# Zero matmuls in thin steps, loads in order of need, stages issued apart from their loads, and an early tail projection in a fused attention and long-convolution kernel

## Chip, cores, metric

One core of one Trainium2 chip runs the whole program. The metric is device time in microseconds (us), median of several executions. A span is the time from the first to the last instruction of the profiled execution; the measured time stands some 2 us above it.

Engines: PE does matmuls, ACT (ScalarE) exponentials, DVE (VectorE) copies out of the accumulators and small arithmetic, POOL (GpSimd) builds convolution operands, SP issues most DMAs. In these traces each starts its work in program order; that is why one wait can hold up what stands behind it (the prediction shows PE for 15.73 us at a convolution matmul, with the next scores behind it).

## The reference, cut

Two independent halves whose outputs are put side by side.

```python
# A: gated long convolution, S = 2048, D = 640
kv = shift(k, 4 taps) * v
y  = causal_convolution(kv, ssm_k) + kv * ssm_D      # by FFT in the reference
a  = q * y
# B: softmax attention, 32 heads of 20
qkv = x @ wqkv
p   = softmax(q @ k.T * 20**-0.5)
b   = (p @ v) @ wo
```

## The kernel before

One loop of 512 steps carries attention. A step `b` handles four heads (group `g`), one of 16 key blocks and one quarter of the queries: scores of four heads by four small matmuls, two exponentials of 128x1024, and PV, four matmuls that accumulate in one bank (`OBANK`) over 16 key blocks. Everything else is fitted into the holes of PE: transposes of x (`X`), the K, Q and V projections, normalisation (`N`), output projection (`T`, `O`), and the convolution as Toeplitz matmuls. All these share one bank, `MISC`, after the first steps.

```python
for b in range(NB):
    EXP_task(b)                                  # two exponentials on ACT
    if b + 1 < NB: S_task(b + 1)                 # scores; first runs the K and Q they need
    if b == 3: late[0] = 2                       # from here all filler uses bank MISC
    for m in (...[b - 1]): PV_task(m)            # first runs the V it needs
    bal = min(bal + (1.4 if b < 24 else 0.9), 1.2)
    if conv is None and kv_over and not any(e[3][0] in "XKV" for e in pend):
        conv_setup(); conv = conv_iter()         # issues loads, first use in the same step
    ... run pending tasks by deadline, else convolution matmuls, while bal lasts ...
    if b >= 6: micro(2)                          # kv product, later output stage A, on DVE
PV_task(NB - 1)
while pend: run_best()                           # tail: normalise, transpose, project, store
```

```python
def A_iter(B):                                   # output stage of the convolution
    A_load(B, 0); A_load(B, 1)
    for tp in range(8):
        ... DVE: Akv * D, + Y, * q ; store ; A_load(B, tp + 2)
```

Loads at the start: four tiles of x on SP, and beside them on ACT's queue the first 160 columns of each weight.

The softmax here doesn't subtract the row's maximum and nothing guards it: scores larger than these inputs give would overflow.

## Time and profile before

| | before |
|---|---|
| median of the first 3 runs | 1043.92 us (1041.96 to 1046.35) |
| span | 1040.8 us |
| mean granted clock of PE | 0.869 |
| first exponential starts | 17.75 us |
| last exponential ends, to the end of the span | 17.7 us |
| holes between exponentials, above 0.916 us from start to start | 67.2 us |

The last three rows and the undisturbed 938 us of exponentials make up the span. The mean clock counts time before the first clock record (24.5 us here) as full, though the transposes there run at the slow pace (20 in 2.31 us). The holes are worked out from the starts of the 1024 exponentials in the trace; the prediction shows the views.

### The profile page before, as it was taken

The page shows a single profiled execution, that of the slowest core. Times are in us where ns is not written, and L with a number is a line of the kernel's source. Part 1 is how long each engine was busy: PE and PEld are TensorE (multiplying, and loading weights), DVE is VectorE, ACT ScalarE, POOL GpSimd, SP SyncE. Part 2 cuts the span into 40 slices and gives each one's busy share as a digit, 9 for nine tenths or more (in the row PEclk, how much of TensorE's full clock was granted, in tenths as well). Part 3 has the DMA queues.
Part 4 walks back from the last instruction along what each step waited for, and adds up shares of the span by engine and source line. Part 5 has one row for each costly group of instructions (what it writes and reads, how often), then busy time and mean ns, then how long its engine had stood idle before and what let it go on. Part 6 is the DMA issues. An engine that isn't in the chain of part 4 may idle for free.

```text
span 1040.8 us, 25021 instructions
## 1 busy us (share of the span) xinstructions
PE 815.2 (78%) x11344; PEld 393.6 (38%) x11344; DVE 266.9 (26%) x568; ACT 949.9 (91%) x1033; POOL 119.1 (11%) x97
## 2 busy tenths in 40 slices
PE   5787888783887888988895888888888887666665
PEld 3332332221543555444452455544453553111112
DVE  3367776220112111121114311121112113200001
ACT  3579999993999999999997999999999999999994
POOL 3000000004220222220222022212220200000000
PEclk9679999996899999899998999999998997555556
DMA  9224443009880988563987578755573673100000
GB/s 353 75 90 144 159 142 112 4 1 145 178 189 31 204 188 182 126 137 94 199 199 181 144 180 191 170 132 134 128 171 91 137 174 98 46 1 1 1 1 26
DMA packets 74758, 129.05 MB, mean 124 GB/s; under 512 B 25729, under 2 KB 51451, under 8 KB 74651
## 3 DMA queue, kind: packets, MB, share of 16 engines
q1 hardware_dynamic: 71979, 124.09, 49.1%
q0 software_dynamic: 704, 2.74, 0.6%
q8 instruction: 89, 1.46, 0.6%
q10 hardware_dynamic: 1968, 0.61, 0.2%
q14 instruction: 18, 0.15, 0.1%
HBM read 116.81 MB, written 13.23 MB: 125 GB/s over the span
## 4 chain that ended last, share of the span: by engine, by line
ACT 76%; PE 15%; DVE 4%; DMA 2%; issue 1%; SPq 1%; POOL 1%; ACTq 0%
ACT P_sb L427 76%; PE PS L309 4%; PE PS L415 4%; PE PS L440 2%; PE PS L596 2%; PE PS L516 1%; PE PS L329 1%; DVE OT_sb L448 1%; DMA R<-in_B_wqkv_dram 1%; PE PS L461 1%; DMA R<-kvr_scratch 1%; DMA R<-kv_scratch 1%; SPq L144 1%; POOL R L573 1%; PE PS L289 0%
## 5 line engine op out<-in xcount | busy, mean ns | idle before, releaser
L427 ACT ACTIVATE P_sb<-PS 128x1024 bf16<-128x1024 f32 x1024 | 944.0, 1176 | 70.6 <-PE PS L415 67.4
L415 PE MATMUL PS<-QT,KT 20*128 20x512 bf16 x2048 | 227.3, 434 | 159.4 <-ACT P_sb L427 146.8
L596 PE MATMUL PS<-R 128*128 128x128 bf16 (+15 forms) x5120 | 219.8, 195 | 18.4 <-POOL R L573 15.7
L440 PE MATMUL PS<-P_sb,V_sb 128*21 128x512 bf16 x2048 | 226.4, 434 | 1.8 <-ACT P_sb L427 1.2
L596 PEld LDWEIGHTS PS<-R 128*128 128x128 bf16 x5120 | 194.0, 98 | 69.1 <-issue 53.1
L415 PEld LDWEIGHTS PS<-QT,KT 20*128 20x128 bf16 x2048 | 52.5, 92 | 295.3 <-ACT P_sb L427 277.8
L573 POOL COPY R<-R 32x512 bf16<-32x512 bf16 x80 | 106.9, 1337 | 473.0 <-PE PS L596 462.1
L440 PEld LDWEIGHTS PS<-P_sb,V_sb 128*21 128x21 bf16 x2048 | 50.5, 89 | 141.4 <-issue 137.2
L609 DVE CAST ZH<-PS 128x256 bf16<-128x256 f32 x40 | 17.0, 424 | 312.0 <-PE PS L596 311.9
L448 DVE CAST OT_sb<-PS 128x512 bf16<-128x512 f32 x32 | 22.1, 690 | 193.1 <-PE PS L440 193.0
L309 PE MATMUL PS<-xT,WQ 128*20 128x512 bf16 x640 | 49.1, 445 | 1.3 <-DVE O_norm L469 0.4
L309 PE MATMUL PS<-xT,R 128*20 128x512 bf16 x640 | 44.4, 411 | 6.1 <-DMA R<-in_B_wqkv_dram 4.1
L317 DVE CAST QT<-PS 128x512 bf16<-128x512 f32 x32 | 22.1, 692 | 57.5 <-PE PS L309 57.5
L329 PE MATMUL PS<-R,xT 128*128 128x160 bf16 (+1 forms) x240 | 34.4, 285 | 2.7 <-DVE V_sb L334 1.4
L317 DVE CAST KT<-PS 128x512 bf16<-128x512 f32 x32 | 22.1, 692 | 49.0 <-PE PS L309 49.0
L516 PE MATMUL PS<-Wo_sb,OnT 128*128 128x320 bf16 x160 | 30.0, 328 | 3.4 <-DVE OnT L507 1.8
L550 POOL MEMSET R<- 128x2048 bf16 x2 | 3.6, 1805 | 224.6 <-PE PS L309 224.5
L329 PEld LDWEIGHTS PS<-R,xT 128*128 128x128 bf16 x240 | 19.5, 108 | 18.7 <-DVE KT L317 4.4
L461 PE MATMUL PS<-ident,OT_sb 128*128 128x128 bf16 x128 | 14.6, 246 | 14.8 <-DVE OT_sb L448 14.8
L623 DVE CAST R<-PS 128x256 bf16<-128x256 f32 x40 | 17.0, 425 | 32.1 <-PE PS L617 32.1
L309 PEld LDWEIGHTS PS<-xT,WQ 128*20 128x20 bf16 x640 | 16.5, 100 | 22.8 <-issue 7.0
L309 PEld LDWEIGHTS PS<-xT,R 128*20 128x20 bf16 x640 | 15.6, 95 | 24.8 <-issue 8.0
(48 smaller groups left out, 285.6 us busy)
## 6 DMA issues: line engine op xcount, KB each, us to landing
R<-kext_scratch SPq DMA_DIRECT2D x320, 264.0 KB, 5.4
R<-in_A_k_dram SPq DMA_DIRECT2D x15, 640.0 KB, 3.8
R<-in_B_x_dram SPq DMA_DIRECT2D x4, 640.0 KB, 7.3
kext_scratch<-in_A_ssm_k_dram POOLq DMA_DIRECT2D x1, 2560.0 KB, 13.4
R<-in_A_v_dram SPq DMA_DIRECT2D x16, 160.0 KB, 5.4
kv_scratch<-R SPq DMA_DIRECT2D x16, 160.0 KB
kvr_scratch<-R SPq DMA_DIRECT2D x16, 160.0 KB
R<-kvr_scratch SPq DMA_DIRECT2D x8, 320.0 KB, 7.0
```

The costliest lines, as they stand in the source:

```text
L309: ins = e.matmul(bank[bk][32 * i:32 * i + DH, :], Wt[:, cc, off + i * DH:off + (i + 1) * DH], xT[:, cc, c * 512:(c + 1) * 512], start=(cc ...
L317: P.op("dve", lambda e: e.tensor_copy(dst, bank[bk]), reads=[bkb[bk]], writes=[bd])
L329: ins = e.matmul(bank[bk][:, 0:w], xT[:, cc, kb * 128:(kb + 1) * 128], WKV[:, cc, D + h0 * DH:D + h0 * DH + w], start=(cc == 0), stop=(cc ...
L415: ins = e.matmul(bank[bk], KT[32 * u:32 * u + DH, g, kb * 128:(kb + 1) * 128], QT[32 * u:32 * u + DH, qc % 2, g, :], start=True, stop=True ...
L427: P.op("act", lambda e, pr=pr, s0=s0: e.activation(P_sb[:, pr % NPS, :], PS[:, s0 * 512:s0 * 512 + 1024], ACT.Exp, scale=scale), reads=[bk ...
L440: ins = e.matmul(bank[OBANK][32 * u:32 * u + DH + 1, :], V_sb[:, kb, 4 * g + u, :], P_sb[:, (2 * b + u // 2) % NPS, (u % 2) * 512:(u % 2) ...
L448: P.op("dve", lambda e: e.tensor_copy(OT_sb[:, i, :], bank[OBANK]), reads=[bkb[OBANK]], writes=[b_OT[i]])
L461: ins = e.transpose(bankh[bk][:, qt * 128:(qt + 1) * 128], OT_sb[:, i, qt * 128:(qt + 1) * 128], ident)
L516: ins = e.matmul(bank[bk][:, 0:320], OnT[:, i, cc, :], Wo_sb[:, cc, hf * 320:(hf + 1) * 320], start=(cc == 0), stop=(cc == NCC - 1))
L573: P.op("pool", lambda e, dst=dst, src=src: e.tensor_copy(dst, src), reads=[cv["KVr"]], writes=[cv["KVX"][i]] if X == 3 else [], extra=(cv[ ...
L596: P.op("pe", lambda e, o=o, lhsT=lhsT, rhs=rhs, st=st, last=last: e.matmul(o, lhsT, rhs, start=st, stop=last, skip_group_check=True), read ...
L609: P.op("dve", lambda e: e.tensor_copy(zh, z1), reads=[bkb[MISC]], writes=[bz[0]])
```

## The change

It means to keep ACT at exponentials: by a warm clock (zeros), an earlier start (loads), loads issued well before the stage that uses them, and a short tail.

```diff
-        P.op("dve", lambda e: e.memset(bank[MISC], 0.0), writes=[bkb[MISC]])   # and three more banks
+        P.op("dve", lambda e: e.memset(Zt, 0.0), writes=[b_Zt])
+        def zeros(bk, n, start):
+            for _ in range(n):
+                P.op("pe", lambda e: e.matmul(bank[bk], Zt, zrhs, start=start, stop=start, ...), ...)
+        for bk in (7, 6, 0, 1, 2, 3, 4, 5, 7, 6):
+            zeros(bk, 1, True)
...
+        x_load(0)
+        w_load("act", 0, 160, b_Wa)
+        # x1 waits for the first weights; then x2, x3, the other weights
...
+        # tail: T tasks of the last quarter early with 4 of 5 chunks; tail_tasks() holds only
+        # the last PV, the last N, one chunk of transposes, and the projections
...
         def A_iter(B):
             A_load(B, 0)
             A_load(B, 1)
+            for _ in range(12):
+                yield
...
-            add(-10 if t < 4 else (t - 4) // 5, 0.45, ("X", t), ...)
+            add(-10 if t < 4 else (t - 4) // 2 if t < 8 else t - 6, 0.4, ("X", t), ...)
...
-            add(max(kb - 1, 2), 0.4, ("V", kb, 0), ...)
+            add(max(kb, 2), 0.41, ("V", kb, 0), ...)
...
+            if b < 40 and pend and min(pend)[2] < 0.45 and min(pend)[0] <= b + 6:
+                run_best()                       # one short task ahead of PV
...
-                conv = conv_iter()
+                conv, conv_b = conv_iter(), b + 10
...
-            if b >= 6:
+            if b >= 5 and stream < 0.35 and (b - 1) % NKB != NKB - 1:
+                zeros(OBANK, 2, False)
+            if b >= 18:
                 micro(2)
```

`stream` is the scheduler's own guess of how long PE streams filler in this step. There are 312 zero matmuls of 128x128 by 128x512: 10 at the start, 302 in the loop.

More of the change, by code (lines that the diff above doesn't have):

```diff
@@ L181, in build_kernel @@
         O_norm = sb("O_norm", [128, 4, D])
-        OnT = sb("OnT", [128, 2, NCC, 128])
+        OnT = sb("OnT", [128, 4, NCC, 128])
+        Zt = sb("Zt", [128, 128])
         Bout = sb("Bout", [128, 2, D])
@@ L239, in build_kernel @@
         b_On, b_rden = Buf(), [Buf(), Buf()]
-        b_OnT = [Buf(), Buf()]
+        b_OnT = [Buf() for _ in range(4)]
+        b_Zt = Buf()
         b_Bo = [Buf(), Buf()]
@@ L250, in build_kernel, with x_load, w_load @@
              reads=[b_ident], writes=[b_ident])
-        P.op("dve", lambda e: e.memset(bank[MISC], 0.0), writes=[bkb[MISC]])
-        P.op("dve", lambda e: e.memset(bank[0], 0.0), writes=[bkb[0]])
-        P.op("dve", lambda e: e.memset(bank[1], 0.0), writes=[bkb[1]])
-        P.op("dve", lambda e: e.memset(bank[OBANK], 0.0), writes=[bkb[OBANK]])
-        for n in range(4):
-            P.dma("sp", xst[n], ap(x2, [[D, 128], [128 * D, 4], [1, D]], n * 512 * D), DS("x%d" % n),
-                  writes=[b_xst[n]])
-        for eng, c0, w, bw in (("act", 0, 160, b_Wa), ("sp", 160, 480, b_Wb)):
+        P.op("dve", lambda e: e.memset(Zt, 0.0), writes=[b_Zt])
+        zrhs = ap(Zt, [list(Zt.ap[0]), [0, 4], [1, 128]])
+        def zeros(bk, n, start):
+            for _ in range(n):
+                P.op("pe", lambda e: e.matmul(bank[bk], Zt, zrhs, start=start, stop=start, skip_group_check=True),
+                     reads=[b_Zt], writes=[bkb[bk]], tok=start)
+        for bk in (7, 6, 0, 1, 2, 3, 4, 5, 7, 6):
+            zeros(bk, 1, True)
+        def x_load(n):
+            return P.dma("sp", xst[n], ap(x2, [[D, 128], [128 * D, 4], [1, D]], n * 512 * D), DS("x%d" % n),
+                         writes=[b_xst[n]])
+        def w_load(eng, c0, w, bw):
             P.dmas(eng, [(ap(t, [list(t.ap[0]), [t.ap[1][0], NCC], [1, w]], o + c0),
@@ L264, in build_kernel @@
                    DS("w" + eng), writes=[bw])
+        x_load(0)
+        w_load("act", 0, 160, b_Wa)
+        P.op("sp", lambda e: e.dma_start(xst[1], ap(x2, [[D, 128], [128 * D, 4], [1, D]], 512 * D)),
+             writes=[b_xst[1]], dsem=DS("x1"), extra=b_Wa.w)
+        x_load(2)
+        t_x3 = x_load(3)
+        w_load("sp", 160, 480, b_Wb)
         rot = [0]
@@ L395, in setup_pool @@
                 ap(kext, [[5 * KXL, 128], [KXL, 5], [1, KPAD]]),
-                ap(tB, [list(tB.ap[0]), [KPAD, 5], [1, KPAD]])), reads=[b_tB], writes=[b_kext], dsem=d_kext)
+                ap(tB, [list(tB.ap[0]), [KPAD, 5], [1, KPAD]])), reads=[b_tB], writes=[b_kext], dsem=d_kext,
+                extra=[t_x3])
             P.op("pool", lambda e: e.dma_start(
@@ L456, in N_task @@
             i = g % 2
-            bk = mbank2()
+            bk = MISC
             def pe(e):
@@ L472, in N_task @@
                 reads=[bkb[bk], b_rden[i]], writes=[b_On])
-            if g == NG - 1:
+            if g == NG - 2 and qc == NQC - 1:
+                for qt in range(4):
+                    add(NB - 12 + 2 * qt, 0.4, ("T", qc, qt), lambda qt=qt: OnT_task(qc, qt, 0, 4))
+            if g == NG - 1 and qc < NQC - 1:
                 b0 = (qc + 1) * 128
@@ L479, in N_task, with OnT_task @@
                             lambda qt=qt, hf=hf: O_task(qc, qt, hf))
-        b_OnT4 = [b_OnT[0], b_OnT[1]]
-        d_B = [DS("b0"), DS("b1")]
-        def OnT_task(qc, qt):
-            if qt >= 2:
+        d_B = [DS("b%d" % i) for i in range(4)]
+        def OnT_task(qc, qt, c0=0, c1=NCC):
+            if qc > 0:
                 for hf in range(2):
-                    ensure(("O", qc, qt - 2, hf))
-            elif qc > 0:
-                for hf in range(2):
-                    ensure(("O", qc - 1, qt + 2, hf))
-            i = qt % 2
-            bk = mbank2()
+                    ensure(("O", qc - 1, qt, hf))
+            bk = MISC
             def pe(e):
-                for cc in range(NCC):
+                for cc in range(c0, c1):
                     ins = e.transpose(bankh[bk][:, cc * 128:(cc + 1) * 128], O_norm[:, qt, cc * 128:(cc + 1) * 128],
@@ L499, in OnT_task @@
             P.op("pe", pe, reads=[b_On, b_ident], writes=[bkb[bk]])
-            evac(OnT[:, i, :, :], bankh[bk][:, 0:640].rearrange("p (c n) -> p c n", c=NCC), bk, b_OnT[i])
+            evac(OnT[:, qt, c0:c1, :], bankh[bk][:, c0 * 128:c1 * 128].rearrange("p (c n) -> p c n", c=c1 - c0), bk,
+                 b_OnT[qt])
         def evac(dst, src, bk, bd):
@@ L507, in evac, with O_mm, pe, O_store @@
                 P.op("dve", lambda e: e.tensor_copy(dst, src), reads=[bkb[bk]], writes=[bd])
+        def O_mm(qt, hf, bk, c0=0, c1=NCC):
+            def pe(e):
+                for cc in range(c0, c1):
+                    ins = e.matmul(bank[bk][:, 0:320], OnT[:, qt, cc, :], Wo_sb[:, cc, hf * 320:(hf + 1) * 320],
+                                   start=(cc == 0), stop=(cc == NCC - 1), skip_group_check=True)
+                return ins
+            P.op("pe", pe, reads=[b_OnT[qt], b_Wo], writes=[bkb[bk]])
+        def O_store(qc, qt, src, bd):
+            P.dma("sp", ap(out2, [[2 * D, 128], [1, D]], (qc * 512 + qt * 128) * 2 * D + D), src, d_B[qt], reads=[bd])
         def O_task(qc, qt, hf):
@@ L511, in O_task, with tail_tasks @@
             i = qt % 2
-            bk = mbank2()
+            O_mm(qt, hf, MISC)
+            evac(Bout[:, i, hf * 320:(hf + 1) * 320], bank[MISC][:, 0:320], MISC, b_Bo[i])
+            if hf == 1:
+                O_store(qc, qt, Bout[:, i, :], b_Bo[i])
+        def tail_tasks():
+            qc, g = NQC - 1, NG - 1
+            tail[0] = True
+            for hf in range(2):
+                O_mm(0, hf, 2 + hf, 0, 4)
+            PV_task(NB - 1)
+            for hf in range(2):
+                O_mm(1, hf, 4 + hf, 0, 4)
+            ensure(("N", qc, g))
+            for hf in range(2):
+                O_mm(2, hf, hf, 0, 4)
             def pe(e):
-                for cc in range(NCC):
-                    ins = e.matmul(bank[bk][:, 0:320], OnT[:, i, cc, :], Wo_sb[:, cc, hf * 320:(hf + 1) * 320],
-                                   start=(cc == 0), stop=(cc == NCC - 1))
-                return ins
-            P.op("pe", pe, reads=[b_OnT[i], b_Wo], writes=[bkb[bk]])
-            evac(Bout[:, i, hf * 320:(hf + 1) * 320], bank[bk][:, 0:320], bk, b_Bo[i])
-            if hf == 1:
-                P.dma("sp", ap(out2, [[2 * D, 128], [1, D]], (qc * 512 + qt * 128) * 2 * D + D), Bout[:, i, :], d_B[i],
-                      reads=[b_Bo[i]])
-        tail = [False]
-        def mbank2():
-            if tail[0]:
-                rot[0] += 1
-                return (MISC, 0, 1, 2, 3, 4, 5)[rot[0] % 7]
-            return MISC
+                for qt in range(4):
+                    ins = e.transpose(bankh[OBANK][:, qt * 128:(qt + 1) * 128], O_norm[:, qt, 512:640], ident)
+                return ins
+            P.op("pe", pe, reads=[b_On, b_ident], writes=[bkb[OBANK]])
+            P.op("dve", lambda e: e.tensor_copy(OnT[:, :, 4, :],
+                                                bankh[OBANK][:, 0:512].rearrange("p (t n) -> p t n", t=4)),
+                 reads=[bkb[OBANK]], writes=b_OnT)
+            for qt, bks, c0 in ((0, (2, 3), 4), (1, (4, 5), 4), (2, (0, 1), 4), (3, (MISC, OBANK), 0)):
+                Bt, bd = P_sb[:, qt, 0:D], b_P[qt]
+                for hf in range(2):
+                    O_mm(qt, hf, bks[hf], c0, NCC)
+                    evac(Bt[:, hf * 320:(hf + 1) * 320], bank[bks[hf]][:, 0:320], bks[hf], bd)
+                O_store(qc, qt, Bt, bd)
+        tail = [False]
         cv = {}
@@ L679, in build_kernel @@
         for t in range(NKB):
-            add(-10 if t < 4 else (t - 4) // 5, 0.45, ("X", t), lambda t=t: XT_task(t))
+            add(-10 if t < 4 else (t - 4) // 2 if t < 8 else t - 6, 0.4, ("X", t), lambda t=t: XT_task(t))
         for g in range(NG):
@@ L687, in build_kernel @@
         for kb in range(NKB):
-            add(max(kb - 1, 2), 0.4, ("V", kb, 0), lambda kb=kb: V_task(kb, 0))
+            add(max(kb, 2), 0.41, ("V", kb, 0), lambda kb=kb: V_task(kb, 0))
             add(18 + kb, 0.4, ("V", kb, 1), lambda kb=kb: V_task(kb, 1))
@@ L718, in build_kernel @@
         S_task(0)
-        conv, conv_over = None, False
+        conv, conv_over, conv_b = None, False, NB
         locked = False
@@ L724, in build_kernel @@
         bal = 0.0
+        stream = 0.0
         def micro(n):
@@ L740, in build_kernel @@
                 late[0] = 2
+            bal = min(bal + (1.3 if b < 24 else 0.9), 1.2)
+            nm, stream = 0, 0.0
+            if b < 40 and pend and min(pend)[2] < 0.45 and min(pend)[0] <= b + 6:
+                run_best()
+                bal -= 0.4
             for m in ([] if b < 3 else [2 * b - 6, 2 * b - 5] if b < 5 else [b - 1]):
                 PV_task(m)
-            bal = min(bal + (1.4 if b < 24 else 0.9), 1.2)
             if conv is None and kv_over and not any(e[3][0] in "XKV" for e in pend):
                 conv_setup()
-                conv = conv_iter()
-            nm = 0
+                conv, conv_b = conv_iter(), b + 10
             if not locked:
-                while pend and nm < (6 if b < 3 else 2 if b < 16 else 1) and (bal > 0.5 or b < 3):
+                while pend and nm < (2 if b < 16 else 1) and bal > 0.4:
                     if min(pend)[0] > b + (40 if b < 128 else 10):
                         break
-                    bal -= run_best()
+                    c = run_best()
+                    bal -= c
+                    stream += 0.8 * c
                     nm += 1
-            if nm == 0 and conv is not None and not conv_over:
+            if nm == 0 and b >= conv_b and not conv_over:
                 while bal > 0:
@@ L762, in build_kernel @@
                         bal -= r
+                        stream += 0.7 * r
                     elif r == "wait":
@@ L767, in build_kernel @@
                         bal -= 0.5
+                        stream += 0.4
                         if r[1] in (19, 39):
@@ L770, in build_kernel @@
                         break
-            if b >= 6:
+            if b >= 5 and stream < 0.35 and (b - 1) % NKB != NKB - 1:
+                zeros(OBANK, 2, False)
+            if b >= 18:
                 micro(2)
-        PV_task(NB - 1)
-        tail[0] = True
-        while pend:
-            run_best()
-        if conv is None:
-            conv_setup()
-            conv = conv_iter()
-        for r in conv:
-            if isinstance(r, tuple) and r[1] in (19, 39):
-                acts.append(A_iter(r[1] // 20))
-        while acts:
-            micro(1)
-        fin = [d[2] for d in d_B + d_ao if len(d) > 2]
+        assert not [e for e in pend if e[3] != ("N", 3, 7)] and conv_over and not acts
+        tail_tasks()
+        fin = [d[2] for d in d_B + d_ao]
         waits = [(t[2], t[1]) for t in fin]
```

## The prediction

> **What bounds the kernel now.** I first read the page. ScalarE (ACT) is busy in 91% of the span, the chain that ended last lies on its exponentials for 76%, and all 1024 of them are one line.
>
> ```profile
> PE 815.2 (78%) x11344; PEld 393.6 (38%) x11344; DVE 266.9 (26%) x568; ACT 949.9 (91%) x1033; POOL 119.1 (11%) x97
> ...
> ACT  3579999993999999999997999999999999999994
> ...
> PEclk9679999996899999899998999999998997555556
> ...
> L427 ACT ACTIVATE P_sb<-PS 128x1024 bf16<-128x1024 f32 x1024 | 944.0, 1176 | 70.6 <-PE PS L415 67.4
> ```
>
> The tenths of ACT show where it is not full: the first three slices, the tenth, the 22nd and the last. The last column of the exponentials says what it waited for: scores (L415). Undisturbed runs give the real price of one: 168 in 154.45 us, less one instruction's 1.176 at the end, over 167 distances, is 0.918 us start to start (the 1176 ns overlap); shorter runs give 0.912. I use 0.916. So a step of the loop (two exponentials) is 1.83 us, and 1024 exponentials need 1023 x 0.916 + 1.18 = 938 us whatever else happens. The span is 1040.8, so 103 us can be had at most. The timeline of ACT says where they are:
>
> ```profile
> 17.75 3.77 ACT L427 ACTIVATE P_sb<-PS 128x1024 bf16<-128x1024 f32 x4 [9.28 <-PE PS L415]
> 23.88 1.94 ACT L427 ACTIVATE P_sb<-PS 128x1024 bf16<-128x1024 f32 x2 [2.36 <-PE PS L415]
> ...
> 258.58 1.94 ACT L427 ACTIVATE P_sb<-PS 128x1024 bf16<-128x1024 f32 x2 [16.09 <-PE PS L415]
> ...
> 277.63 154.45 ACT L427 ACTIVATE P_sb<-PS 128x1024 bf16<-128x1024 f32 x168 [0.58 <-PE PS L415]
> ...
> 559.99 1.94 ACT L427 ACTIVATE P_sb<-PS 128x1024 bf16<-128x1024 f32 x2 [6.00 <-PE PS L415]
> ```
>
> The first exponential starts at 17.75 and the last ends at 1023.1, so head 17.75, tail 17.7, and between them 1005.3 - 938.2 = 67 us of holes. Summing the excess of each start-to-start distance over 0.916 us by stage: 21.9 us up to 72.6; 6.6 to 240; 16.7 at 258; 2.2 to 278; 4.8 to 549; 7.3 at 560; 4.7 to 875; 3.0 after it (total 67.2).
>
> The two big holes have one shape: PE's queue is in order, and it stands at an instruction whose data has just been asked for, while the next scores stand behind it.
>
> ```profile
> 239.89 5.72 SPq L144 DMA_DIRECT2D R<-kvr_scratch  x4
> 250.71 11.07 POOL L573 COPY R<-R 32x512 bf16<-32x512 bf16 x8 [7.19 <-DMA R<-kvr_scratch]
> 256.26 1.73 PE L596 MATMUL PS<-R 128*128 128x128 bf16 x21 [15.73 <-POOL R L573]
> ...
> 556.91 0.49 DVE L641 TENSOR_TENSOR R<-R,Dbc 128x640 bf16<-128x640 bf16 x1 [7.56 <-DMA R<-kv_scratch]
> ```
>
> Loads of the convolution are issued at 239.9, its copies on GpSimd start at 250.7, its first matmul at 256.3. At 556.9 VectorE, also in order, stood 7.56 us at a load of the output stage; a normalisation and transpose that PE needed were behind it.
>
> The small holes are mostly cold clock. Windows:
>
> ```profile
> 25.00:50.00 25.00, 19.60 (x183) 8.53 (x183) 9.32 (x24) 15.00 (x17) 0.00 (x0) 0.69 0.30 94
> 175.00:200.00 25.00, 19.90 (x292) 6.56 (x288) 9.81 (x18) 25.00 (x29) 0.00 (x0) 1.00 0.05 18
> 900.00:1000.00 100.00, 63.34 (x444) 12.62 (x440) 5.76 (x12) 98.14 (x107) 0.00 (x0) 0.50 0.00 1
> ```
>
> (us; PE, PEld, DVE, ACT, POOL busy; granted clock; DMA share; GB/s.) With a K or Q projection in most steps and the clock at 1.00, ACT has no hole at all (175 to 200). A projection's 20 matmuls span 2.31 us cold and 1.25 warm; cold it alone exceeds a step. At 900 to 1000 the clock is half throughout and ACT is still 98% busy: thin steps (scores and PV, 0.61 us each when cold) do not need the clock.
>
> **The Trainium skill.** "TensorE: Matmul & The Clock Gate", Part 1: the clock has a half and a full rate, judged in free-running windows of 3.4 us of activity, and gaps make it cold. The trace agrees on the rates and windows (cold stretches last 3.41 us or multiples) but not that only idleness counts: taking each matmul as its columns at the granted clock, I find that all 18 drops to half rate follow a window with PE streaming 16 to 45% of the time, and all 18 rises one with 77 to 90%. "PSUM — Partial Sum Buffer", The four PSUM rules: a matmul without the first-flag adds where the bank was written, so zeros leave PV as it is, and one with the flag can take over from the four VectorE memsets; a time trace cannot show values. "ScalarE: Activation LUTs", What ACT_TABLE_LOAD costs: 186 ns + 0.833 per element, 93 ns overlapped, gives 946 ns; the trace's 0.912 to 0.918 is less, and is used. "DMA: Bandwidth & Descriptors", Why small descriptors are slow: small packets move less per unit of time. The DMA view of the first 30 us agrees:
>
> ```profile
> q1 hardware_dynamic: 5306, 6.41, 62.6%
> q10 hardware_dynamic: 1968, 0.61, 8.1%
> ```
>
> Of 16 x 30 us, a packet of q10 (the first weights, 320 B each by their shape) takes 20 ns, one of q1 57 ns.
>
> **The change part by part.** From the instruction order of both builds; steps are counted by scores.
>
> *Loads.* Before, x0 to x3 (2.6 MB) share the engines with the first weights (0.6 MB), which end at 11.7 us. Now only x0 does: packet time (512 x 57 + 1920 x 20) / 16 = 4.2 us, begun at about 2, so they land near 7 (estimate). x0's 20 transposes take 5.4 to 7.7 and their copies to 8.5 as before, and now gate. Then K and Q: 4.45 us cold, 2.3 warm, plus 1.46 from Q's end to the first exponential. The ten zero matmuls (about 1.2 to 5.5, cold 0.427 each) may warm the clock: 12.2 warm, 14.4 cold; I take 13.0. **Gain 4.8.**
>
> *Early steps (to about step 30).* The kv product on VectorE starts 12 steps later, x transposes are spread, and zeros lift a thin warm step from 0.43 to 0.85 us of streaming per 1.83, 46%: just over the 45% at which the last drop happened; cold they make 1.71, 93%, enough to rise. I go through steps 3 to 29 with warm durations: scores and PV 0.33 each to the next issue, projection 1.1, V about 0.33, zeros 0.43, and 0.45 or 0.76 where PE waits for a V or K copy. Step 7 has V, wait, PV, transposes, zeros, then K for the very next scores and its copy: about 4.0 us against 1.83, a hole of 2. Steps 4, 5 and 11 lose about 1 each, other steps to 10 about 0.5, and 13, 14, 16, 19, 24, 29 (V and a projection) about 0.6. With the slack of about 0.3 us in a step that is 13. **Gain 9.**
>
> *Clock elsewhere.* Half of the zeros lie after step 432, where only the boundary steps lose (0.46 us each): gain 1.5. Holes of 1.2 us at cold projections from 72 us on should shrink: 6.6 to 2, 2.2 to 0.5, 4.8 to 1.5, 4.7 to 1.5. **Gain 14.3 with the end.**
>
> *Convolution.* Loads, clearing and copies are issued 10 steps, 18.3 us, before the first matmul; the chain needed 16.4 (239.84 to 256.26). **Gain 15.7**, leaving 1.
>
> *Output stage.* 12 rests at two per step are 11 us, the load took 7.1. **Gain 6.3.**
>
> *Tail.* Now four of five transposes and projections per row tile stand ready. From the last exponential: PV 0.5, copy 0.7, one more projection holding PE (to 1.5), transposes 0.4, reciprocal and multiply 0.85, transposes and copy 1.1, then 16 matmuls and eight copies of 0.44 to 0.49 on two engines to about 7.2, and the 2.2 us that the store and the end took before: 9.5. **Gain 8.2.**
>
> Sum: 4.8 + 9 + 14.3 + 15.7 + 6.3 + 8.2 = 58.3. The other way: 13.0 + 938.2 + 22 of holes (13 + 2 + 1 + 0.5 + 1.5 + 1 + 1.5 + 1.5) + 9.5 = 982.7 of span; the median stands 3.1 above the span, so 985.8.
>
> **Rivals.** *Zeros make PE the bound.* 302 zeros in the loop at 0.43 us cold are at most 130 us of PE. A cold thin step becomes 0.54 + 0.54 + 0.86 = 1.94 us against 1.83. If the clock flickers there, 151 steps lose up to 0.1: 15 us back, about 1000. Against: the step itself rises to 93%. *Early stage stays bound by waits.* The steps before 12 still put V right before the PV that needs it; if the clock stays cold there the 9 us shrink to about 0: 995. *The wait moves.* Ten steps leave only 2 us of margin for the loads; a slower load shows a few us of hole: 990. Conversely, if early steps hide the copies better than I think: 975. *Nothing gained because ACT sets the pace anyway:* against it speaks that the 67 us are holes in ACT itself.
>
> **Range and chances.** The convolution, output stage and tail (30 us) follow from single visible waits and are nearly sure; head and clock (28 us) may come at a third or at full with something over. So 974 to 1003. Faster by 2% needs 1023: all but certain.
>
> **What would show it.** Right: first exponential at 12 to 14.5; no hole over 3 us at the convolution or output stage; granted clock near 1.0 after 880 us; zero matmuls outside every chain; last exponential to end 9 to 10.5. Wrong: a clock of 0.5 to 0.8 with zeros present, ACT's distance in steady runs above 0.92, or early holes above 18 us.

## The result

The changed kernel took 1000.98 us (993.27 to 1006.58, 4 runs), the kernel before 1043.59 us in the same rounds: ratio 0.9584, 95% interval 0.9504 to 0.9664. (A ratio is the mean time of one kernel's runs over that of the other's of the same rounds, so not quite the ratio of the medians.) The span of the profiled run is 994.7 us. The time lies inside the predicted range, 15 us above the predicted figure, and its spread of 13 us is new: the kernel before spreads by 4 us here and by 5 to 7 in the sets below.

The page of the changed kernel, the same lines as before (PE as a whole, ACT and granted clock in 40 slices, the exponentials):

```profile
PE 834.1 (84%) x11656; PEld 398.7 (40%) x11656; DVE 266.8 (27%) x568; ACT 947.5 (95%) x1031; POOL 118.9 (12%) x97
...
ACT  4578999999999999999999999999999999999996
...
PEclk7799999999999999999999999999999999999989
...
L446 ACT ACTIVATE P_sb<-PS 128x1024 bf16<-128x1024 f32 x1024 | 943.4, 1239 | 34.6 <-PE PS L434 29.7
```

ACT is full from the fifth slice to the last but one, and the clock is high everywhere but at the start. What is left is the start: its tenths, 4 5 7 8, are no better than before (3 5 7 9). The timeline of ACT shows it (start, duration, what; idle time before, and who ended it):

```profile
11.01 7.44 ACT L446 ACTIVATE P_sb<-PS 128x1024 bf16<-128x1024 f32 x8 [3.68 <-PE PS L434]
22.53 1.94 ACT L446 ACTIVATE P_sb<-PS 128x1024 bf16<-128x1024 f32 x2 [4.09 <-PE PS L459]
...
40.37 1.94 ACT L446 ACTIVATE P_sb<-PS 128x1024 bf16<-128x1024 f32 x2 [4.49 <-PE PS L434]
42.78 1.94 ACT L446 ACTIVATE P_sb<-PS 128x1024 bf16<-128x1024 f32 x2 [0.47 <-PE PS L434]
...
195.32 343.42 ACT L446 ACTIVATE P_sb<-PS 128x1024 bf16<-128x1024 f32 x374 [0.20 <-PE PS L434]
...
544.90 415.24 ACT L446 ACTIVATE P_sb<-PS 128x1024 bf16<-128x1024 f32 x452 [0.33 <-PE PS L434]
```

The first exponential starts 6.7 us sooner. Then come holes of up to 4.5 us until 40 us, and of 0.2 to 1.6 us, mostly about 0.5, in most steps until 95. From 195 us on, the 374 and 452 exponentials of the two stretches shown run almost without a hole; the holes of 16 and 6 us are gone.

Holes by steps (sum of the excess over 0.916 us, from the trace):

| steps | before | changed | what lies there |
|---|---|---|---|
| 0 to 30 | 22.7 | 28.1 | x, first K, Q, V |
| 30 to 96 | 4.4 | 4.6 | more K, Q, V |
| 96 to 110 | 18.0 | -0.2 | start of the convolution |
| 110 to 256 | 7.1 | 0.2 | convolution |
| 256 to 290 | 7.1 | 0.8 | first output stage |
| 290 to 432 | 4.9 | 0.2 | convolution |
| 432 to 512 | 3.0 | 2.2 | scores and PV alone |
| all | 67.2 | 35.9 | |

With the first exponential (17.75 to 11.01) and the tail (17.7 to 9.4) this is 6.7 + 31.3 + 8.3 = 46.3, and the span fell by 46.1.

**The convolution.** Timeline lines from SP, POOL and PE, the same events as before:

```profile
217.37 5.66 SPq L144 DMA_DIRECT2D R<-kvr_scratch  x4
...
229.96 11.09 POOL L615 COPY R<-R 32x512 bf16<-32x512 bf16 x8 [8.98 <-DMA R<-kvr_scratch]
...
236.04 1.35 PE L638 MATMUL PS<-R 128*128 128x128 bf16 x33
```

The chain is no shorter, 12.6 us from issue to first copy (10.8 before) and 18.7 to the first matmul (16.4 before), but PE no longer stands in it: its matmul line names no wait. It was close: the first tile's four copies end at 235.46 in the trace, 0.6 us before PE arrives.

**The output stage.** The waits of DVE for this load (total, times, longest):

```profile
DVE R L685 <- DMA R<-kv_scratch: 13.5, 11, 2.5
```

Before, the longest was 7.56 us; 2.5 does not reach ACT.

**The start.** Timeline of the first weights' user and what it waited for:

```profile
5.26 1.29 PE L307 MATMUL PS<-ident,R 128*128 128x128 bf16 x20 [0.22 <-DMA R<-in_B_x_dram]
...
7.06 0.39 SPq L278 DMA_DIRECT2D R<-in_B_x_dram  x1
...
7.43 1.26 PE L327 MATMUL PS<-xT,R 128*20 128x512 bf16 x20 [0.88 <-ACT xT L315]
```

The second x tile is issued at 7.06, when the first weights have landed (before, they were waited for until 11.84), and the first projection then waits for copies of x, not for weights. It takes 1.26 us, so the clock is warm.

**The tail.**

```profile
985.72 0.40 PE L459 MATMUL PS<-P_sb,V_sb 128*21 128x512 bf16 x4
...
987.14 0.39 PE L480 MATMUL PS<-ident,OT_sb 128*128 128x128 bf16 x4
...
988.88 0.42 DVE L563 COPY OnT<-PS 128x512 bf16<-128x512 bf16 x1 [0.53 <-PE PS L560]
...
991.74 0.49 DVE L525 CAST P_sb<-PS 128x320 bf16<-128x320 f32 x1 [0.21 <-PE PS L530]
```

The last exponential ends at 985.3, the last copy at 992.2, the span at 994.7: 9.4 us.

**The clock.** Windows (us; PE, PEld, DVE, ACT, POOL busy; granted clock; DMA share; GB/s) of the changed kernel:

```profile
16.00:39.00 23.00, 20.01 (x143) 8.07 (x139) 5.11 (x12) 10.20 (x11) 0.68 (x1) 0.51 0.82 274
39.00:64.00 25.00, 19.73 (x235) 8.19 (x231) 8.10 (x18) 17.72 (x19) 0.00 (x0) 1.00 0.00 1
850.00:950.00 100.00, 71.16 (x550) 17.49 (x550) 10.22 (x21) 99.74 (x110) 0.00 (x0) 0.95 0.07 19
```

Late, the clock is 0.95, where the kernel before has 0.60 in the same stretch and the changed kernel without the loop's zeros (second run below) 0.50. Early, from 15 to 39 us, it is half, and ACT is busy for 10.2 of 23 us. Even from 39 to 64 us, with the clock full, ACT is busy in only 17.7 of 25 us. So two theories for the early holes: the cold clock, or waits that any clock has. Around 28 us PE, DVE and PE again do this:

```profile
26.86 0.85 PE L347 MATMUL PS<-R,xT 128*128 128x160 bf16 x5
27.75 0.33 DVE L352 CAST V_sb<-PS 128x160 bf16<-128x160 f32 x1 [0.94 <-PE PS L347]
28.13 0.61 PE L459 MATMUL PS<-P_sb,V_sb 128*21 128x512 bf16 x4 [0.42 <-DVE V_sb L352]
```

V is projected right before the PV that reads it, and PE stands still until DVE has copied it. The page adds this up:

```profile
L459 PE MATMUL PS<-P_sb,V_sb 128*21 128x512 bf16 x2048 | 206.2, 393 | 4.2 <-DVE V_sb L352 4.2
```

In the kernel before PV waited for V's copy once, for 0.4 us; here ten times, for 4.2 us in all. The change itself is the likely maker: it put V's deadline one step later (`kb - 1` became `kb`). No run alters this alone.

### The profile page after: what moved, and what is told of

The parts are those of the page before. It is cut to its first block, busy times and chain, and to the rows that moved or that the text cites. A ratio compares the mean times of both kernels' runs of the same rounds, so it can differ in the third digit from the quotient of the medians.

```text
span 994.7 us, 25641 instructions
## 1 busy us (share of the span) xinstructions
PE 834.1 (84%) x11656; PEld 398.7 (40%) x11656; DVE 266.8 (27%) x568; ACT 947.5 (95%) x1031; POOL 118.9 (12%) x97
## 4 chain that ended last, share of the span: by engine, by line
ACT 83%; PE 10%; DVE 4%; DMA 1%; issue 1%; SPq 0%
ACT P_sb L446 83%; PE PS L327 3%; PE PS L434 2%; PE PS L347 2%; PE PS L459 1%; PE PS L259 1%; DVE V_sb L352 1%; DVE KT L335 1%; PE PS L530 1%; PE PS L307 1%; DMA R<-kv_scratch 1%; DVE OT_sb L467 0%; DMA R<-in_B_x_dram 0%; PE PS L480 0%; DVE R L387 0%
## 5 line engine op out<-in xcount | busy, mean ns | idle before, releaser
L434 PE MATMUL PS<-QT,KT 20*128 20x512 bf16 x2048 | 205.4, 391 | 126.6 <-ACT P_sb L446 113.4
L638 PE MATMUL PS<-R 128*128 128x128 bf16 (+15 forms) x5120 | 214.5, 193 | 2.6 <-DVE QT L335 1.2
L459 PE MATMUL PS<-P_sb,V_sb 128*21 128x512 bf16 x2048 | 206.2, 393 | 4.2 <-DVE V_sb L352 4.2
L638 PEld LDWEIGHTS PS<-R 128*128 128x128 bf16 x5120 | 189.1, 97 | 51.1 <-issue 51.1
L259 PE MATMUL PS<-Zt 128*128 128x512 bf16 x312 | 99.5, 405 | 1.0 <-DVE Zt L253 1.0
L327 PE MATMUL PS<-xT,R 128*20 128x512 bf16 x640 | 42.0, 393 | 2.6 <-ACT xT L315 0.9
L327 PE MATMUL PS<-xT,WQ 128*20 128x512 bf16 x640 | 41.2, 387 | 1.0 <-DVE O_norm L488 0.4
L259 PEld LDWEIGHTS PS<-Zt 128*128 128x128 bf16 x312 | 21.0, 100 | 26.9 <-issue 25.9
L530 PE MATMUL PS<-Wo_sb,OnT 128*128 128x320 bf16 x160 | 26.6, 301 | 0.7 <-DVE OnT L563 0.5
L352 DVE CAST V_sb<-PS 128x160 bf16<-128x160 f32 (+1 forms) x48 | 18.3, 382 | 24.8 <-PE PS L347 24.0
```

What stands on the lines that cost most here:

```text
L259: P.op("pe", lambda e: e.matmul(bank[bk], Zt, zrhs, start=start, stop=start, skip_group_check=True), reads=[b_Zt], writes=[bkb[bk]], tok=s ...
L327: ins = e.matmul(bank[bk][32 * i:32 * i + DH, :], Wt[:, cc, off + i * DH:off + (i + 1) * DH], xT[:, cc, c * 512:(c + 1) * 512], start=(cc ...
L352: P.op("dve", lambda e: e.tensor_copy(V_sb[:, kb, h0:h0 + nh, 0:DH], bank[bk][:, 0:w].rearrange("p (h d) -> p h d", d=DH)), reads=[bkb[bk] ...
L434: ins = e.matmul(bank[bk], KT[32 * u:32 * u + DH, g, kb * 128:(kb + 1) * 128], QT[32 * u:32 * u + DH, qc % 2, g, :], start=True, stop=True ...
L459: ins = e.matmul(bank[OBANK][32 * u:32 * u + DH + 1, :], V_sb[:, kb, 4 * g + u, :], P_sb[:, (2 * b + u // 2) % NPS, (u % 2) * 512:(u % 2) ...
L530: ins = e.matmul(bank[bk][:, 0:320], OnT[:, qt, cc, :], Wo_sb[:, cc, hf * 320:(hf + 1) * 320], start=(cc == 0), stop=(cc == NCC - 1), skip ...
```

## The experiments

Twelve runs in three sets, each set on one chip with its own runs of the kernel before (medians 1041.95, 1042.71 and 1041.18 us). Between sets I compare ratios, at 10.4 us to one hundredth.

**First set.** The changed kernel again.

> The changed kernel unaltered, as the baseline of this set and to see its spread (993 to 1007 us in four runs, granted clock 0.983 to 0.952 falling as the time rises). Theory (cold clock early): the time is set by how long the clock stays at half in steps 0 to 30; the profiled run lost 28 us there with 24 us cold. Expected 993 to 1007 us again, and a profile whose early holes are 18 to 35 us, larger the longer the early cold stretch. Rival (waits alone): early holes 28 us within 2, whatever the cold stretch, and the spread lies elsewhere.

995.66 us (991.70 to 1003.85, 6 runs), ratio 0.9554. Its profile has early holes of 26.6 us with the clock cold from 14 for 20 us. The spread is there again, 12 us.

The loop's zeros taken out:

```diff
-            if b >= 5 and stream < 0.35 and (b - 1) % NKB != NKB - 1:
-                zeros(OBANK, 2, False)
```

> The changed kernel without the 302 zero matmuls of the loop (the ten at the start stay). If the zeros hold the clock: granted clock falls from 0.976 to about 0.87, holes of 1 us return at cold projections and 0.46 us at the last boundaries, together 8 to 16 us: 1009 to 1017 us. Rival (the new order of tasks did it, zeros are idle work): within 3 us of the changed kernel's median, 998 to 1004 us, with the clock low.

1001.1 us (1000.04 to 1003.37), ratio 0.961, clock 0.889: 5.4 us slower than the changed kernel beside it. That misses the 1009 to 1017 that I expected and lies in the rival's 998 to 1004, though the rival allowed only 3 us. The profile says why it is not more. After step 30 the holes are 20.7 us against 7.8 in the changed kernel's first profile, and the tail 11.2 against 9.4 us: together 15 us lost without zeros. But this run had no cold stretch before 121 us, and its early holes are 17.8 instead of 28.1. That was not the plan of the edit: up to step 5 this kernel is the changed kernel, instruction for instruction, and there the clock fell at 14.8 and 14.5 us in two profiles and not at all in this one. So the same code can go either way. It gave the first hint that the cold clock (with the zeros of the early steps) costs some 9 us, and that nearly 18 remain without it.

Zeros in steps 0 to 3:

```diff
-        late[0] = 1
+        late[0] = 2
         S_task(0)
...
+            if b < 4:
+                zeros(OBANK, 3 if b == 0 else 2, False)
```

> The changed kernel with nine more zero matmuls in steps 0 to 3 (three, then two a step) and the transposes of those steps kept to one bank so that the zeros have the other. If the cold clock makes the early holes: the clock stays at 1.0 through steps 0 to 12, the holes of steps 0 to 30 fall from 28 to about 14 us, time 982 to 988 us and the spread of the runs shrinks to under 4 us. Rival (PE waits for the copies of V and K in any clock): holes of 24 us or more, time 995 us or more.

997.45 us (995.90 to 998.50), ratio 0.9569, early holes of 28.3 us: no gain, and by its numbers what the rival said (24 us or more, 995 or more). But it does not test the theory: the clock fell at 13 us, before the first extra zeros ran at 14.7, and the transposes, now in one bank, waited for each other's copies. Inconclusive.

The convolution begun in the step that issues its loads:

```diff
-                conv, conv_b = conv_iter(), b + 10
+                conv, conv_b = conv_iter(), b
```

> The changed kernel with the convolution begun in the step that issues its loads, as before. If the ten steps hide the loads: one hole of about 16 us returns near 240 us less the earlier gain, 1013 to 1019 us. Rival (the loads are hidden anyway, or the earlier order of the queues removed the wait): 998 to 1004 us.

1016.03 us (1014.45 to 1017.84), ratio 0.9749 against 0.9554: 20 us slower, and the hole is back in ACT's timeline:

```profile
231.48 1.94 ACT L446 ACTIVATE P_sb<-PS 128x1024 bf16<-128x1024 f32 x2 [16.22 <-PE PS L434]
```

So the ten steps hide the loads, and are worth these 16 us; the hole also cools the clock (cold from 218 for 17 us).

**Second set.** The rests of the output stage taken out:

```diff
-            for _ in range(12):
-                yield
```

> The changed kernel without the 12 rests between the loads of the output stage and their first use. If the rests hide the load: the hole of about 6 us returns near step 263, holes of steps 256 to 290 rise from 0.4 to about 6.5 us, time up by 6 us against the changed kernel (median 996 to 1001, so 1001 to 1007). Rival (the load is hidden anyway): no change.

1002.44 us (999.97 to 1009.18), ratio 0.9625. The hole is back, once and with a second one behind it:

```profile
529.74 1.94 ACT L446 ACTIVATE P_sb<-PS 128x1024 bf16<-128x1024 f32 x2 [7.38 <-PE PS L434]
...
549.71 1.94 ACT L446 ACTIVATE P_sb<-PS 128x1024 bf16<-128x1024 f32 x2 [2.43 <-PE PS L434]
```

Holes of steps 256 to 290 are 12.3 us in this profile, against 0.8 and 0.0 in two of the changed kernel. (This profile is of the slowest of the four runs.) By ratio, 4 to 7 us. The rests hide the load.

Loads in the old order, the first zeros kept:

```diff
         x_load(0)
-        w_load("act", 0, 160, b_Wa)
-        # x1, waiting for the first weights
+        x_load(1)
         x_load(2)
         t_x3 = x_load(3)
+        w_load("act", 0, 160, b_Wa)
```

> The changed kernel with the loads issued in the old order (four x tiles first, beside the first weights). The first exponential went from 17.75 to 11.0 us. If the order of loads is 4.5 us of this (first weights at 6.9 instead of 11.8 us) and the warm clock for K and Q the other 2.1: first exponential at 15 to 16 us here if the clock is warm then, up to 17.7 if it is cold again after the longer wait; time up by 4 to 7 us, unless the early holes shrink because x is there sooner. Rival (zeros alone moved the first exponential): first exponential at 11 to 13 us.

1000.44 us (995.10 to 1007.11), ratio 0.9599. The first exponential moved to 16.65 us, so the order of loads makes 5.6 of the 6.7 us at the start. The time alone does not show it: this profile happened to have only 7 us of cold clock, half of it before the first exponential, and early holes of 20.6. Measured again below.

An explicit order for steps 0 to 14:

```diff
+        EARLY = {0: ("X4 X5 X6", ""), 1: ("X7 V0 K1", ""), 2: ("V1 V2 X8 X9", ""), 3: ("", "X10 V3"),
+                 4: ("V4", "X11"), 5: ("V5", "K2"), 6: ("V6", "X12"), 7: ("V7", "X13"), ...
+                 12: ("V13", "Q"), 13: ("V14", "K1,0"), 14: ("V15", "")}   # before PV, after PV
...
         S_task(0)
+        zeros(OBANK, 2, False)
```

> The changed kernel with an explicit order of tasks in steps 0 to 14: each V one step ahead of the PV that reads it, K a step or more ahead of its scores, no zeros in those steps but two right after the first scores. If the waits for copies are the larger part of the early holes: holes of steps 0 to 30 fall from about 27 us to 8 to 14, time 979 to 986 us, even in runs whose clock drops early. Rival (the cold clock alone): holes stay near 18 when warm and 27 when cold, 990 to 1000 us.

986.32 us (985.30 to 987.46, 5 runs), ratio 0.9461: faster than the changed kernel by 10 to 13 us by ratio, with a spread of 2, and just outside the 979 to 986 that I expected. Early holes 13.6 us and no cold stretch before 88 us. The V of a later step now goes ahead of PV, and PV waits for nothing:

```profile
28.84 0.52 PE L347 MATMUL PS<-R,xT 128*128 128x160 bf16 x5 [0.26 <-DVE xT L317]
29.29 0.40 PE L459 MATMUL PS<-P_sb,V_sb 128*21 128x512 bf16 x4
```

The order does two things at once, fewer waits and a warm clock, so it alone does not say which counts.

The kernel before with nothing but the loop's zeros:

```diff
+            if b >= 5 and stream < 0.35 and (b - 1) % NKB != NKB - 1:
+                zeros(OBANK, 2, False)
             if b >= 6:
                 micro(2)
```

> The kernel before with nothing but zero matmuls in thin steps of the loop (280 of them by the same rule, none at the start). If zeros are worth the cold holes wherever they are: clock from 0.87 to about 0.95, holes of 72 us and later (outside the two large ones) fall by 10 to 14 us, 1027 to 1033 us. If zeros only pay together with the new order: within 4 us of the kernel before.

1038.17 us (1036.16 to 1039.17), ratio 0.9955: 4.5 us, less than half of the 10 to 14 that I expected and hardly more than the rival's 4. The clock rose to 0.951, holes of the first 30 steps fell from 22.7 to 17.7 and of the last 80 from 3.0 to 0.7, but those of steps 110 to 256 were 10.9 instead of 7.1. In its trace the cold stretches in the middle include those behind the two large holes (237 for 17 us, 551 for 10). Whether these are what spoils the rest was not tested.

**Third set.** The changed kernel's own order, only kept warm:

```diff
         S_task(0)
+        zeros(OBANK, 2, False)
...
+            if b < 3:
+                zeros(OBANK, 2, False)
```

> The changed kernel in its own order, with eight more zero matmuls (two after the first scores, two at the end of each of steps 0 to 2, after the transposes). It separates clock from order: the run without loop zeros happened to be warm early and lost 17.8 us there, the runs that went cold for 20 to 24 us lost 27 to 28. If the clock is its own cause: no cold stretch before 60 us and early holes of 17 to 20 us, time 986 to 990 us with a spread under 4. Rival (only the order counts, the clock just follows the waits): cold again before step 12 and holes of 25 us or more, 994 to 1000 us.

991.03 us (988.90 to 992.98), ratio 0.9513 against 0.9554: 4 us faster than the changed kernel's better set, spread 4; 1 us slower than expected, and the two intervals still touch (0.9488 to 0.9538, 0.9521 to 0.9586), so the time alone settles little. The page and the holes do: no cold stretch before 124 us, and early holes of 20.8.

```profile
ACT  5679999999999999999999999999999999999996
...
PEclk9999999989999999999999999999999998978999
```

So the clock is a cause of its own, worth 6 to 7 us of the early holes. The profiles of other runs that keep this early order and its zeros fit: 28.0 us of holes with 24 us of cold clock in steps 0 to 30 (no rests), 23.2 with 10 (convolution at once), 20.6 with 3 (old loads). And 20.8 remain in a warm clock, where the explicit order has 13.6: the order is the other cause.

Explicit order with three more edits:

```diff
-     8: ("V8", "X14"), 9: ("V9", "X15"), 10: ("V10", "K3")
+     8: ("V8", "X14 X15"), 9: ("V9", "K3"), 10: ("V10", "")
...
                 run_best()
                 bal -= 0.4
+                stream = 0.3                     # the task ahead of PV counts as filler
...
+                    if b >= 432 and (b - 1) % NKB == NKB - 1 and min(pend)[3][0] == "N":
+                        zeros(MISC, 2, True)     # N goes one step later
+                        break
```

> The explicit early order with three more edits: the last K of the first group one step earlier (its copy is waited for 1.7 us now), no zeros in steps that already hold two V products, and in the last 80 steps the normalisation transposes one step later with zeros in their place. If these waits are what is left: early holes 13.6 to about 11, steps 30 to 96 from 6.8 to 4 to 5, the last 80 steps from 2.9 to under 1; time 979 to 983 us against 986 of the explicit order alone. Rival (the loss only moves to the next step): 985 to 988.

982.61 us (980.83 to 983.41, 5 runs), ratio 0.9430, interval 0.9407 to 0.9453: the best version. Its page:

```profile
ACT  6789999999999999999999999999999999999996
...
PEclk9999999999999999999999999999999999999999
```

The last 80 steps lose 0.1 us instead of 2.9. The early steps hardly changed (13.2, not the 11 expected), and steps 30 to 96 fell from 6.8 to 5.8: there most of the loss only moved, as the rival said. K's wait became two smaller ones (ACT idle for 1.08 and 0.84 us in place of 1.71).

Explicit order without the loop's zeros (the edit of the second run):

> The explicit early order without the zeros of the loop (the two after the first scores and the ten at the start stay). A cleaner measure of the zeros than before, as this order's runs spread by only 2 us. If zeros hold the clock and are worth about 14 us outside the early steps: 997 to 1001 us, clock about 0.89. If the gain of the zeros lay in luck of the early clock: 986 to 990.

992.87 us (990.53 to 996.93), ratio 0.9535 against 0.9461: the zeros are worth 7.7 us by ratio, 6.6 by medians, between my two expectations (997 to 1001 if they are worth 14, 986 to 990 if luck). In the same stretch as above, where the explicit order with zeros has a clock of 0.87 and ACT busy for 99.39 us:

```profile
850.00:950.00 100.00, 63.36 (x444) 12.50 (x444) 6.61 (x14) 98.60 (x108) 0.00 (x0) 0.50 0.03 9
```

With the clock at half ACT is still busy in 98.6%. Without zeros the tail is 11.24 instead of 9.40 us, the holes after step 30 are 17.4 instead of 11.9, and the early holes 11.4 instead of 13.6. So the zeros take back 2 us in early steps: up to step 14 the two profiles agree to 0.1 us, and all of it lies in steps 15 to 29.

Explicit order with the old loads (the edit of the sixth run):

> The explicit early order with the loads in the old order: a cleaner measure of the order of loads, whose undoing moved the first exponential of the changed kernel from 11.0 to 16.65 us but not clearly the time. If the loads are worth what they move at the start: 5 to 6 us more than the explicit order, 991 to 993. If later steps give it back (x tiles land sooner, fewer early holes): 986 to 989.

990.34 us (989.44 to 995.55), ratio 0.9517 against 0.9461: 5.8 us by ratio, 4.0 by medians, about what I expected (991 to 993). First exponential at 16.89 against 11.26, early holes 13.6 in both. The 5.6 us at the start stay as a gain; later steps do not give them back.

## Why the prediction was right, and where it was not

The mechanism held: holes in ACT, each with its own cause, and the sum of their removals. By its own steps, predicted against measured gain in the span:

- **Loads and first zeros**: 4.8 against 6.7. The choice of 13.0 between 12.2 (warm) and 14.4 (cold) was too careful: the transposes came out warm too (1.29 instead of 2.31 us), so the first projection began at 7.4 and not at 8.5. The order of loads makes 5.6 (run with the old loads), the clock the rest.
- **Convolution**: 15.7 predicted, and steps 96 to 110 fell from 18.0 to -0.2; undone alone, a hole of 16.22 us returned. The margin was indeed thin (0.6 us).
- **Output stage**: 6.3 predicted; steps 256 to 290 fell from 7.1 to 0.8.
- **Tail**: 9.5 us predicted, 9.4 measured. Some 1.8 of it is clock: 11.2 in both runs without the loop's zeros.
- **Clock elsewhere**: 14.3 predicted. The same stages (all after step 30 but the two large holes) fell from about 22 to 7.8 us, so the sum was right. Taken out of the changed kernel the loop's zeros are worth 12.9 us there (20.7 against 7.8), but out of the explicit order only 5.5 (17.4 against 11.9). In time they are worth 5 to 8 us, since the early steps give back some (2 us in the explicit order) or happen to be warm without them (the second run).
- **Early steps**: this step failed. "I go through steps 3 to 29 with warm durations" and "that is 13. Gain 9" came out as 28.1 and 26.6 us in two profiles, a loss of 4 to 5 us. (The losses that it lists come to 11 rather than 13: one of 2 us, three of 1, five of 0.5, six of 0.6.) Two things were mis-sized. First, the waits and the zeros' own time: in a warm clock the same order loses 20.8 us (the run kept warm), not 13. For steps 12 to 29 I had counted 0.6 us in six steps, and in that trace sixteen of the eighteen lose 0.3 to 1.2, 9.9 us together. Second, the clock: durations were taken as warm because "zeros lift a thin warm step" to 46% of streaming. But the rule puts no zeros before step 5. Steps 0 and 1 hold only scores and the transposes of two x tiles each, and the clock fell there (at 14.8 and 14.5 us) in both profiles. Once cold it stayed so for 20 and 24 us, because a step with waits for V, X and K cannot stream enough to bring it back. By the same reckoning as in the prediction (columns at the granted clock), most windows that stayed cold in the changed kernel streamed 57 to 75%, those after which it rose 75 to 93% (one at the end of the span aside); two cold ones of over 80% show that this is no sharp threshold.

Split by steps, the early holes (us, from the traces) show which cause sits where:

| steps | before | changed, two profiles | kept warm | changed, no loop zeros (warm by chance) | explicit order | the same, no loop zeros |
|---|---|---|---|---|---|---|
| 0 to 3 | 4.2 | -0.1, -0.1 | -0.1 | -0.1 | 0.4 | 0.4 |
| 3 to 8 | 7.4 | 14.8, 13.3 | 7.4 | 7.2 | 2.3 | 2.3 |
| 8 to 15 | 9.4 | 5.9, 5.9 | 5.9 | 5.3 | 4.1 | 4.1 |
| 15 to 30 | 1.7 | 7.5, 7.5 | 7.5 | 5.3 | 6.8 | 4.6 |

The cold clock costs 6 to 7 us, all in steps 3 to 7. The explicit order, which also drops the zeros of steps 5 to 13, takes another 7 us out of steps 3 to 14; the zeros are less than 1 of these (13.3 us kept warm, 12.5 warm without zeros). In steps 15 to 29 the changed kernel loses 5.8 us more than the kernel before: 2.2 are the zeros, and the rest comes with the other edits; with which, no run tested.

This step is nearly the whole miss: by the span, loads gained 1.9 us more than predicted, early steps lost 14.4 against their term, and the rest came out within half a us. Of the 15 us to the predicted time, 12 are this sum. The median also stands 4.5 us above the profiled run, and the 3.1 us that the prediction added from span to time, the median of one run less the span of another, are 1.8 when both are of one run.

The second rival, "Early stage stays bound by waits", with 995 us, is thus what happened, by both its halves and somewhat worse. Three of the prediction's own signs say the same: early holes are above 18 us, the clock stays at half until 39 us though the loop's zeros begin at 32, and the zeros are not outside every chain (1.1% of the chain that ended last, some 11 us). That the total still lies in the range is due to the other terms, which were right. That the order and the clock are separate causes is shown by the run kept warm and the run reordered. The run-to-run spread fits the clock too (mean clock 0.983, 0.976, 0.957 and 0.952 at 993, 996, 1005 and 1007 us), but only one run of each kernel has a profile, so that the extra cold lies in the early steps is not shown. What decides at the start of a run which execution goes cold was not controlled and stays open; so does the question whether the explicit order would stay warm without the two zeros after the first scores.

## What to carry to other kernels

Before counting on a warm clock, list the steps that the warming rule does not reach, and those with waits: a clock that fell can stay low while waits keep PE from streaming enough (here it rose only after windows of about 75% or more). A projection whose result is read next in the same in-order queue costs its copy each time; issue it one step ahead. Put filler work only into steps that have room, and issue loads at least as many steps ahead as the whole chain of load and preparation takes.

## What the Trainium skill lacked or had wrong

- "TensorE: Matmul & The Clock Gate", Part 1: it speaks of idle gaps and of sustained activity, but gives no share of a window. Counted as in the prediction, over the 3.41 us before each change, the clock fell here only after windows in which PE streamed at most 45% (18 times in the kernel before, 7 in the changed one), and rose only after windows of about 75% or more. Neither is a sharp threshold: some ten warm windows of 44% or less in the kernel before were followed by no fall, and two cold ones of over 80% in the changed kernel by no rise. In between, the changed kernel, streaming mostly 57 to 75% without a PE gap over 0.8 us, stayed cold for 24 us. The page also says "Keep TensorE busy ≥4µs continuously" (Why this matters for your kernels), but has no price for filler: here 302 zero matmuls in the loop were worth 5 to 8 us of 1000, and took 2 us where steps were full.
- "ScalarE: Activation LUTs", What ACT_TABLE_LOAD costs: its figures give an estimate of 946 ns from start to start (186 + 853 - 93) for 1024 elements with an immediate scale and bias; undisturbed runs here, out of PSUM, take 912 to 918 ns.
- No page has the price of a matmul right behind the one whose copied result it reads: PE stood still for 0.42 us at V's copy (0.33 us on DVE) and 0.80 us at K's (0.69 us).
